# Reordering one first-transform piece and adding 14 idle products at the seam of a spectral filter and its hash-routed experts

## The chip, the cores and the metric

One core of one Trainium2 chip runs the whole program in one launch. The metric is the device time of that core in microseconds (us), as the median of the runs. Its engines are named as in the profile: PE (matrix products, with PEld for the loading of weights), DVE, ACT and POOL (element-wise work), SP (issue of transfers); ACT and POOL issue transfers as well. All transfers share 16 DMA engines.

## The reference

Eight sequences of 2496 tokens with 256 channels are filtered in the frequency domain; then every token goes through one of eight experts, which its id chooses.

```python
X = np.fft.rfft(x, axis=1)
y = np.fft.irfft(X * (filt_r + 1j * filt_i)[None], n=x.shape[1], axis=1)
x = y.reshape(B * S, D)                       # 19968 tokens, D = 256
expert_idx = token_ids * np.int64(2654435761) % np.int64(E)     # E = 8
for e in range(E):
    xe = x[expert_idx == e]
    out[expert_idx == e] = np.maximum(xe @ w1[e], 0.0) @ w2[e]  # F = 1024
```

All of it is in float32.

## The kernel before

**The filter.** A sequence ("batch", class `Batch`, L219) is transformed by two small discrete transforms, 2496 = 39 x 64. Stage 1 (`stage1`, L280) multiplies pieces of the input by a table `wf_t`; there are six pieces (u = 0 to 5) of four columns each, the last one shorter. A piece is four matrix products of 256 columns into two PSUM tiles "pa" (`products`, L253), each followed by an ACT copy to a slot of `mid` (L269). Only the second piece of a pair (u = 1, 3) writes its pair to DRAM (`d`, L297), and for the third and fourth batch that write can be put off (list `put_off`, L293). Stage 2 loads `d` again (`load2`, L299), multiplies by a second table ("pb", L312), by the filter on DVE (L318 to L323) and by the way back ("pc", L335). Stage 3 (`stage3`, L417) makes the last products "pd" (L261, L267), which ACT copies to a tile `o`, and POOL then scatters the rows of `o` to their expert's place in the DRAM array `xs` by indirect DMA (`scatter`, L432). The first two batches turn their data on PE instead of going through DRAM (`turn4`, L382, "pu" and the DVE copies "t", L398 and L401).

**The experts.** The rows of `xs` are worked off in blocks of 256 tokens. `load` (L835) gathers a block by four transfers `xg` and one transfer `no` of the row numbers; for block 0 SP issues three of them and ACT two, for block 1 SP issues all, later blocks are ACT's. DVE transposes the block (`token_parts`, L852, "xt") and makes sums ("st", L868). `up` (L880) has 28 products of 128 columns into the banks a, b, c with DVE sums and ACT activations ("ht", L891) between them; `down` (L917) has 16 products of 256 columns ("dps", L922). `up` asks for the block after the next one right after its first ACT copy (L899, `ask`): the five transfers of that block stand in ACT's queue ahead of the four activations. The first block may start when all rows of the first two batches lie in `xs`.

**What sets the order.** The order is written out by hand: every piece of work has a due time in a list, the list is sorted (L819), and the pieces with a negative time, here `head` less 200 (L797), run ahead of the experts. Each engine then runs its own instructions strictly in that order, with waits on semaphores where one engine needs another. Around the change the list is: third batch's stage 1 with its last pieces at 119 and 121 (L789), second batch's last piece of stage 3 (u = 5) at 123 (L788), fourth batch's first four pieces of stage 1 at 123 to 123.3 (L796), `begin` at 123.5 and the loads of blocks 0 and 1 at 123.6 (L790), the put-off writes of the third batch at 124 (L791), its `load2` at 125 (L792), the put-off writes of the fourth batch at 126 (L794). A transfer counts on one of eight semaphores ("lanes") of its kind, in the order of the list as built, and an issue that takes a lane waits until the transfer that had the lane before has landed.

`warm` (L757) exists before as well: it is called once at the program's very start and multiplies the identity by itself into bank a.

```python
def warm(n):
    ps = banks["a"].tile([P, 4, P], F32, name="warm", tag="a")
    for k in range(n):
        nc.tensor.matmul(out=ps[:, k % 4, :], lhsT=ident[:], rhs=ident[:], start=True, stop=True)
```

Of the kernel before, what the change touches and what calls it, by code (L numbers as in the profile page):

```python
# [125 lines left out]
def kernel(  # L126
# [630 lines left out]
# [6 lines that stand above are left out]
    third = batches[2]  # L763
    head = [(0, lambda: warm(14))]
# [28 lines left out]
    fourth = batches[3]  # L793
    head += [(126, lambda: [nc.sync.dma_start(out=dram, in_=chip) for dram, chip in put_off[3]])]  # L794
    head += [(t, lambda v=v: fourth.load1(v)) for v, t in enumerate((113, 113.1))]
    head += [(123 + .1 * u, lambda u=u: fourth.stage1(u)) for u in range(4)]  # L796
    todo = [(t - 200, piece) for t, piece in head]  # L797
    todo += [(t, lambda k=k: pads(k)) for k, t in enumerate((10.9, 11.6, 11.9, 16.9, 17.6, 17.95, 22.9))]

# [16 lines left out]
    for e in range(E):  # L816
        t = 34.3 + 1.5 * e
# [313 lines left out]
```

## Time and profile before

| what | value |
|---|---|
| three runs | 1421.33, 1423.53, 1431.88 us; median 1423.53 us |
| the profiled execution | 1424.24 us, its span 1422.5 us |
| PE busy | 1373.4 us (97% of the span) |
| PEld busy | 1273.3 us (90%) |
| DVE, POOL, ACT busy | 890.2, 830.3, 416.6 us |
| mean granted clock of PE | 0.99 |
| chain that ended last | 86% PE, 8% DMA, 3% DVE |
| PE busy from 100 to 150 us | 42.55 of 50 us, granted clock 0.93 |
| PE busy from 150 to 175 us | 21.91 of 25 us, granted clock 0.86 |
| PE busy from 250 to 325 us | 75 of 75 us, granted clock 1.00 |

How to read it: times in the views are us from the start of the span. A timeline line gives start, duration, engine, line, operation, "output<-input" and, in brackets, how long the engine was idle before it and what ended that. An fp32 product shows as two records, so "x8" is four products. "PEclk" and the clock column are the share of its full speed that PE was granted: 1.00 or 0.50, or a mean over a slice with both.

### The profile page before, as it was taken

How to read it: one execution, taken by the hardware profiler on the slowest of the kernel's cores; microseconds unless marked ns; L12 is line 12 of the kernel's file. 1: busy time of each engine (PE TensorE's matmuls, PEld its weight loads, DVE VectorE, ACT ScalarE, POOL GpSimd, SP SyncE). 2: the span in 40 equal slices, each digit the busy share in tenths (PEclk: the TensorE clock that was granted, in tenths of full speed). 3: DMA queues.
4: the chain of work that ended last, by engine and by line, in shares of the span. 5: the costliest groups of instructions: out<-in, count | busy, mean ns of one | idle time of the engine just before them, and what ended most of it. 6: DMA issues, size and time to landing. Idle time of an engine off the chain costs nothing.

```text
span 1422.5 us, 26307 instructions
## 1 busy us (share of the span) xinstructions
PE 1373.4 (97%) x9398; PEld 1273.3 (90%) x9398; DVE 890.2 (63%) x1636; ACT 416.6 (29%) x760; POOL 830.3 (58%) x736
## 2 busy tenths in 40 slices
PE   7898999999999999999999999999999999999997
PEld 7776888989888988889999899999999999999997
DVE  7773575575556566445665477657766776676775
ACT  4554122223232223232222222222222222222222
POOL 6167243844665565578533587788855566555563
PEclk9999899999999999999999999999999999999999
DMA  8677765757987698888755785887742526261611
GB/s 222 206 235 216 212 218 121 260 192 245 269 270 224 183 284 264 261 262 273 241 167 131 219 258 170 235 242 235 254 138 68 190 62 199 46 218 42 215 46 35
DMA packets 244505, 278.33 MB, mean 196 GB/s; under 512 B 125171, under 2 KB 213670, under 8 KB 234948
## 3 DMA queue, kind: packets, MB, share of 16 engines
q1 hardware_dynamic: 95149, 179.33, 40.2%
q10 hardware_dynamic: 129303, 52.69, 15.4%
q0 software_dynamic: 19920, 44.59, 8.9%
q8 instruction: 77, 1.26, 0.4%
q14 instruction: 56, 0.46, 0.1%
HBM read 293.65 MB, written 86.15 MB: 267 GB/s over the span
## 4 chain that ended last, share of the span: by engine, by line
PE 86%; DMA 8%; DVE 3%; issue 1%; ACT 1%; ACTq 0%; SPq 0%; POOLq 0%; POOL 0%; DVEq 0%
PE dps L922 22%; PE up_b L887 9%; PE up_a L887 6%; PE up_c L887 6%; PE pd L267 5%; PE pb L312 4%; PE dnc L949 4%; PE dnb L949 4%; PE dna L949 4%; PE upc L944 4%; PE upa L944 4%; PE pc L335 3%; PE pa L267 3%; DMA t<-d 2%; PE upe L944 2%; PE upb L944 2%
## 5 line engine op out<-in xcount | busy, mean ns | idle before, releaser
L922 PE MATMUL dps<-wts,ht 128*128 128x256 f32 x1600 | 370.9, 382 | 6.1 <-ACT ht L891 6.1
L922 PEld LDWEIGHTS dps<-wts,ht 128*128 128x128 f32 x1600 | 304.7, 192 | 50.6 <-ACT ht L891 7.3
L1014 POOL DMA_INDIRECT out_dram<-osb,no x158 | 165.2, 1046 | 219.2 <-DVE osb L956 137.8
L433 POOL DMA_INDIRECT xs<-o,sidx x176 | 177.0, 1006 | 168.7 <-ACT o L269 73.3
L877 POOL TENSOR_TENSOR tw<-wts 128x512 f32<-128x512 f32 x158 | 205.1, 1298 | 116.0 <-DMA wts<-in_moe_w_dram 92.4
L877 POOL TENSOR_TENSOR tw<-wts,tw 128x512 f32<-128x512 f32 x158 | 206.1, 1305 | 6.2
L894 DVE TENSOR_TENSOR ht<-up_b,ht 128x512 f32<-128x512 f32 x150 | 103.7, 691 | 114.6 <-PE up_b L887 91.2
L891 ACT ACTIVATE ht<-ht 128x512 f32<-128x512 f32 x150 | 94.3, 630 | 188.8 <-DVE ht L894 164.9
L322 DVE TENSOR_TENSOR z<-pb,filt 64x512 f32<-64x512 f32 x160 | 110.2, 689 | 30.9 <-PE pc L335 28.9
L927 DVE COPY osb<-dps 128x512 f32<-128x512 f32 x50 | 34.6, 691 | 150.2 <-PE dps L922 149.7
L887 PE MATMUL up_a<-xt,wts 128*128 128x128 f32 x800 | 115.3, 277 | 9.1 <-DVE xt L855 4.9
L887 PEld LDWEIGHTS up_a<-xt,wts 128*128 128x128 f32 x800 | 105.9, 193 | 12.7 <-DVE xt L855 5.3
L887 PE MATMUL up_b<-st,tw 128*128 128x128 f32 x800 | 107.4, 278 | 2.7 <-DVE ht L894 1.8
L887 PEld LDWEIGHTS up_b<-st,tw 128*128 128x128 f32 x800 | 98.1, 193 | 4.9 <-issue 3.7
L953 ACT ACTIVATE ht<-ht 128x512 f32<-128x512 f32 x90 | 56.6, 630 | 122.1 <-DVE ht L956 75.8
L894 DVE TENSOR_TENSOR ht<-up_c,ht 128x512 f32<-128x512 f32 x100 | 69.0, 690 | 37.2 <-PE up_c L887 32.4
L338 ACT COPY mid<-pc 128x512 f32<-128x512 f32 x60 | 35.0, 584 | 154.8 <-PE pc L335 91.5
L267 PE MATMUL pd<-t,wi_t 120*117 120x256 f32 x320 | 77.5, 385 | 2.6 <-DMA t<-d 2.6
L318 DVE TENSOR_TENSOR y<-pb,filt 128x512 f32<-128x512 f32 x80 | 55.1, 689 | 37.8 <-PE pb L312 35.6
L269 ACT COPY o<-pd 117x512 f32<-117x512 f32 x80 | 45.0, 585 | 104.4 <-DMA xg<-xs 45.4
L312 PE MATMUL pb<-mid,d_t 128*128 128x256 f32 x280 | 74.1, 388 | 1.1 <-DVE z L322 1.1
L898 ACT COPY ht<-up_a 128x512 f32<-128x512 f32 x50 | 29.3, 587 | 150.6 <-PE up_a L887 120.7
(210 smaller groups left out, 2466.1 us busy)
## 6 DMA issues: line engine op xcount, KB each, us to landing
wts<-in_moe_w_dram SPq DMA_DIRECT2D x162, 1024.0 KB
xg<-xs ACTq DMA_DIRECT2D x321, 64.0 KB
mid<-d SPq DMA_DIRECT2D x70, 256.0 KB
d<-mid ACTq DMA_DIRECT2D x60, 256.0 KB
d_t<-t2s SPq DMA_DIRECT2D x15, 1024.0 KB
e_t<-t2s SPq DMA_DIRECT2D x15, 1024.0 KB
x<-in_x_dram SPq DMA_DIRECT2D x39, 312.0 KB
t<-d SPq DMA_DIRECT2D x12, 960.0 KB
```

The costliest lines, as they stand in the source:

```text
L267: nc.tensor.matmul(out=ps[0:cols * H, k, :], lhsT=w[:], rhs=src[:, 2 * i + k, :], start=True, stop=True)
L312: nc.tensor.matmul(out=ps[:, i, :], lhsT=d_t[:, s, :], rhs=rhs, start=True, stop=True)
L322: nc.vector.tensor_tensor(out=z[b], in0=ps[a], in1=f_t[1][64 * hi:64 * hi + 64, s1:s1 + 2, :], op=OP.mult)
L433: st = nc.gpsimd.indirect_dma_start(out=xs[:], out_offset=bass.IndirectOffsetOnAxis(ap=index, axis=0), in_=rows, in_offset=None, bounds_ch ...
L877: eng.tensor_tensor(t[k][:], p, q, op=OP.subtract)
L887: nc.tensor.matmul(out=ps[bank][:, f, :], lhsT=w[:, f * P:(f + 1) * P], rhs=xx, start=first and f == 0, stop=True, skip_group_check=True)
L891: nc.scalar.activation(out=out, in_=in_, func=AF.Relu)
L894: nc.vector.tensor_tensor(out, ps[bank][:], other, op=OP.add)
L922: nc.tensor.matmul(out=ps[:, h, :], lhsT=ht[:, h, fp, :], rhs=w2[:, fp, :], start=(fp == 0), stop=(fp == FP - 1))
L944: nc.tensor.matmul(out=ps[:, f, :], lhsT=w[:, f * P:(f + 1) * P], rhs=xx, start=first and f == 0, stop=True, skip_group_check=True)
L949: nc.tensor.matmul(out=ps[:, 0, :], lhsT=a[:, f, :], rhs=b[:, f, :], start=first and f == 0, stop=True, skip_group_check=True)
L1014: st = nc.gpsimd.indirect_dma_start(out=out[:], out_offset=bass.IndirectOffsetOnAxis(ap=to_rows[i][:, h:h + 1], axis=0), in_=o[:, h, :], i ...
```

## The change

The first piece of the fourth batch's stage 1 gets the due time 121.5, ahead of the second batch's last piece of stage 3 at 123; the other three keep their order at 123.1 to 123.3. After them, still ahead of `begin`, stand 14 products of `warm`.

```diff
     head += [(t, lambda v=v: fourth.load1(v)) for v, t in enumerate((113, 113.1))]
-    head += [(123 + .1 * u, lambda u=u: fourth.stage1(u)) for u in range(4)]
+    head += [(t, lambda u=u: fourth.stage1(u)) for u, t in enumerate((121.5, 123.1, 123.2, 123.3))]
+    head += [(123.4, lambda: warm(14))]
     todo = [(t - 200, piece) for t, piece in head]
```

As built, PE has the four products of the piece ahead of the two of "pd" and 14 more ahead of the first "up_a"; ACT has the piece's two copies ahead of the two copies of `o`; DVE, POOL and SP have the same instructions in the same order. Ten of the 1286 transfers stand in the list, or count on a lane, otherwise than before: four in which two scatters of POOL and two input loads of SP change places in the list without a change of lane, and six around the gather of block 2. There the third and fourth transfer `xg` of block 2 and its `no` have other lanes: `no` counts on the lane of the first put-off write of the third batch (L791), where before it counted on that of block 2's own first `xg`.

## Prediction

> **What bounds the kernel now.** I read the page's busy shares and slices first:
>
> ```profile
> PE 1373.4 (97%) x9398; PEld 1273.3 (90%) x9398; DVE 890.2 (63%) x1636; ACT 416.6 (29%) x760; POOL 830.3 (58%) x736
> PEclk9999899999999999999999999999999999999999
> ```
>
> PE is the bound almost everywhere, so only idle or half-clocked PE time can be won, and only near the seam from 100 to 180 us, where a slice shows 8. There, second, the timeline of PE:
>
> ```profile
> 126.99 1.21 PE L261 MATMUL pd<-t,wi_t 120*117 120x256 f32 x4 [1.77 <-DVE t L401]
> 128.13 8.85 PE L267 MATMUL pa<-x,wf_t 117*120 117x256 f32 x32
> 141.85 2.08 PE L887 MATMUL up_a<-xt,wts 128*128 128x128 f32 x8 [4.87 <-DVE xt L855]
> ...
> 153.09 10.02 PE L922 MATMUL dps<-wts,ht 128*128 128x256 f32 x32 [3.12 <-ACT ht L891]
> ```
>
> Three gaps: 1.77, 4.87 and 3.12 us. Each is followed by slow products: "dps" took 10.02 us for 32 records, where full speed is 16 records in 3.45 us (chain, at 201.84), so 6.9. Third, one-microsecond windows (columns: stretch; PE, PEld, DVE, ACT, POOL busy; granted clock; DMA share; GB/s):
>
> ```profile
> 128.00:129.00 1.00, 1.00 (x3) 0.77 (x3) 0.87 (x4) 0.63 (x2) 0.69 (x2) 0.58 0.56 204
> 131.00:132.00 1.00, 1.00 (x5) 0.81 (x4) 1.00 (x2) 0.16 (x1) 0.70 (x2) 0.71 0.35 99
> ...
> 141.00:142.00 1.00, 0.15 (x1) 0.15 (x1) 0.88 (x2) 0.00 (x0) 1.00 (x2) 0.91 0.78 137
> 145.00:146.00 1.00, 1.00 (x9) 1.00 (x9) 0.39 (x1) 0.00 (x0) 0.00 (x0) 0.88 1.00 292
> ...
> 152.00:153.00 1.00, 0.00 (x0) 0.00 (x0) 0.37 (x2) 1.00 (x3) 0.00 (x0) 0.53 0.46 42
> 158.00:159.00 1.00, 1.00 (x4) 0.82 (x3) 0.00 (x0) 0.00 (x0) 0.00 (x0) 0.55 1.10 308
> ```
>
> From the fractions the clock is half from 128.17 to 131.58, 141.82 to 145.24 and 152.06 to 158.89: one, one and two steps of 3.41 us on one fixed grid. Judged by grid steps: 124.75 to 128.17 was 48% busy and a drop followed; 134.99 to 138.41 was 59% busy (work until 137.0) and none followed; 148.65 to 152.06 was 39% busy, a drop. So a step that is about half idle drops the clock, and a full step of work at half clock restores it.
>
> Fourth, what releases the first block ("up_a" at 141.85)? POOL's timeline and SP's:
>
> ```profile
> 135.26 0.90 POOL L433 DMA_INDIRECT xs<-o,sidx  x1 [0.30 <-ACT mid L269]
> 137.55 3.32 SPq L844 DMA_DIRECT2D xg<-xs  x7
> ```
>
> POOL scatters back to back, every 1.30 us, until 136.2; the last lands at 137.4 by the trace's DMA updates, SP gathers block 0 from 137.55, DVE transposes at 141.08. PE has no part in it. Fifth, what releases "dps" at 153.09? ACT's timeline:
>
> ```profile
> 144.18 5.53 ACTq L844 DMA_DIRECT2D xg<-xs  x4
> 151.47 0.40 ACTq L844 DMA_DIRECT2D no<-xs  x1
> 151.92 0.63 ACT L891 ACTIVATE ht<-ht 128x512 f32<-128x512 f32 x1 [7.37 <-DMA xg<-xs]
> ```
>
> The four activations stand behind block 2's `no`, which is not issued until 151.47 although its predecessor's issue ended at 149.71: it waits for its lane, whose last transfer, block 2's first `xg`, landed at 151.45.
>
> [...]
>
> **The change, part by part.**
>
> *The moved piece:* four products (1.73 us at full clock, as at 122.34) and two ACT copies of 0.59; no DMA, as only odd pieces write. PE ends the third batch's stage 1 at 125.22. The piece's input, the fourth batch's first x load, landed only at 126.40 by the DMA updates, so it runs from about 126.45 to 128.2, not from 125.22. "pd" was ready at 126.99 and now starts at 128.2: 1.2 us late. Behind "pd" are ACT's two copies of `o`, before at 128.24, now about 129.5, and behind those POOL's last two scatters at 133.97 and 135.26. Slack 133.97 - 130.1 = 3.9 us, so this costs nothing; the cover is POOL's backlog of scatters, and without it the cost is the 1.2 us. ACT's copies of `o` also pass the piece's two copies, 1.2 us, inside that slack. No queue of SP, DVE or POOL is passed.
>
> *The clock there:* the step 124.75 to 128.17 becomes 0.47 + 1.72 = 2.19 busy, 64%: no drop, 1.7 us of PE saved. Three pieces remain: 129.2 + 3 x 1.73 = 134.4 (their input x, landed by about 130.4, is in time at 130.9). Before: 137.0.
>
> *The 14 products:* eight records of this shape take 0.89 us ("up_b", chain), so 28 take 3.12: 134.4 to 137.5. They wait for nothing; bank a was free since the copies at 117.8. They end where PE ended before (137.0), 4.3 us ahead of "up_a". Cost nothing: they lie in the wait for POOL. Without that cover, 3.1.
>
> *The first block:* "up_a" still at 141.85. An idle stretch of 4.3 us leaves some grid step over half idle wherever the grid lies (at best 2.15 on each side, 63% of a step). So "up" is cold as before, end at 149.97. Gain to here: 0.
>
> *The lane:* as built, `no` of block 2 now waits for the first put-off write, which landed at 148.31, not for the `xg` landing at 151.45. Issue then at 149.75, after the fourth `xg`, 1.72 us sooner; activations at 150.2; "dps" at 151.37. The step 148.65 to 152.06 is then 1.32 + 0.69 busy, 59%: on the edge, as the step that did not drop. No drop makes "dps" 6.9 instead of 10.02, 3.1 more. PE stands 1.7 to 4.8 us ahead at the end of "dps".
>
> *What takes it back:* the fourth batch's fifth piece (L267, at 176.58) needs x loaded by SP:
>
> ```profile
> 176.58 1.96 PE L267 MATMUL pa<-x,wf_t 117*120 117x256 f32 x8 [0.31 <-issue]
> ```
>
> PE waited for x there already: the third x transfer landed at 176.38. It was issued at 173.15, when block 4's first `xg`, its lane's predecessor, had landed (173.13); the second at 170.36, when a put-off write of the fourth batch had landed (170.34), which PE doesn't move. With PE ahead that `xg` is issued up to 4.8 us earlier, so the third goes right behind the second, at 171.2, and with the same 3.2 us lands at 174.4: "pa" at 174.6, 2.0 us sooner. The rest of the lead becomes idle time: 176.27 - 4.8 = 171.5, so up to 3.1 us idle, over half of a step, and a new drop costs up to 3.41/2 = 1.7. Unknown bounds here: the third x may land at 174.4 (lead 2.0) or,[...] at 176.4 (lead 0). Later DVE stalls on the chain (0.85 at 187.79, 0.47 at 209.78) may shrink with a DVE that started earlier: 0 to 0.9 more. From 250 us on PE has no gap to hide in, so the lead at 240 reaches the end.
>
> Sum: lead 2.0, less half of the possible 1.7 for the drop (I can't tell from the edge case which), rounded with the DVE relief left out: 1.2 us. 1422.5 - 1.2 = 1421.3 of span; with 1.74 around it (1424.24 - 1422.5) 1423.0 for that execution. It stands 0.71 above the median 1423.53, so **1422.3** as a median.
>
> **Rivals.**
> *A. The products keep the clock up* through "up" and "dps": 1.7 + 3.4 less at the first block, and x in time too. For it: the drops at 141.82 and 152.06 are real. Against: 4.3 us idle after them. If POOL's chain came in about 2.5 us sooner it would hold. Time 1423.5 - 5 = 1418.5.
> *B. Slower: the lead turns into a cold stretch.* Place: the wait for the fifth piece's x. PE comes at 171.5, x stays at 176.4, the step 172.54 to 175.96 is empty, the clock drops. Price 1.7 us with nothing won: 1425.2. It decides once the wait exceeds half a step, 1.7 us, while x lands after 176. For it: x landing is paced by writes of the fourth batch, not by PE. Against: its third part has a lane that PE's lead frees.
> *C. Late "pd" holds the scatters.* It decides if x lands after 126.4 + 3.9 = 130.3; each us beyond is one us more, 1425 at 132. Against: 3.9 us of slack.
> *D. Nothing reaches the end*: the built order does move the piece, but all of it lies in waits, and the lane's 1.7 us goes into the wait for x: 1423.5.
>
> **How the numbers follow.** Forecast 0.45, A 0.12, B 0.2, C 0.05, D 0.18. About 1%, 14 us, is what a measurement of this kernel can tell from no change; all cases lie within 5 us. [...]each drop is 1.7 us, and the three runs shown spread from 1421.33 to 1431.88. The forecast's own range is 1420 to 1425; with A, B and that spread 1417.5 to 1427.5. Faster by over 1%: 0.01; within: 0.97; slower: 0.02.
>
> **What would show it.** In the profile after: no idle over 1.3 us at 125, "pd" about 1.2 us later, no half clock at 128 (grid permitting); the idle products ending near 137.5; "up_a" with 4 to 5 us idle before it, then half clock; POOL's last scatter at 135; `no` of block 2 issued right after its fourth `xg`; "dps" at about 151.4; a longer wait ahead of the fifth "pa". I am wrong if "up" runs at full clock from its start, if SP's gather of block 0 moves by over 1 us, or if PE's lead at 240 us exceeds 3 us.

## The result and the profile after

In its first measurement the changed kernel took 1418.74 us (median of 20 runs, 1412.59 to 1425.83) beside 1425.16 for the kernel before (20 runs): ratio 0.995, interval [0.9929, 0.9971]. A second measurement, on another occasion, gave 0.9974 [0.9956, 0.9992]. So it is 0.26 to 0.5% faster, some 4 to 7 us. (The ratios in this document, with their 95% intervals, are not the quotients of the medians beside them.) The forecast was 1.2 us. The gain is real, and most of it is not where the forecast looked.

The page of the profile after has PE's busy time 4.1 us lower, although 28 matmul and 28 weight-load records more are in it:

```profile
PE 1369.3 (97%) x9426; PEld 1271.4 (90%) x9426; DVE 891.9 (63%) x1636; ACT 416.0 (29%) x760; POOL 828.0 (59%) x736
PEclk9999999999999999999999999999999999999999
```

**At the seam** nearly every step went as written. PE's timeline after, from the moved piece on:

```profile
124.00 1.99 PE L267 MATMUL pa<-x,wf_t 117*120 117x256 f32 x8
125.82 1.15 PE L261 MATMUL pd<-t,wi_t 120*117 120x256 f32 x4
126.90 5.44 PE L267 MATMUL pa<-x,wf_t 117*120 117x256 f32 x24
132.18 3.29 PE L761 MATMUL warm<-ident 128*128 128x128 f32 x28
138.78 1.40 PE L888 MATMUL up_a<-xt,wts 128*128 128x128 f32 x8 [3.31 <-DVE xt L856]
...
148.09 7.17 PE L923 MATMUL dps<-wts,ht 128*128 128x256 f32 x32 [0.91 <-ACT ht L892]
```

The 1.77 us gap is gone, the idle products end 3.3 us ahead of "up_a", and "dps" waits 0.91 us instead of 3.12 and takes 7.17 us instead of 10.02. The reason for the shorter wait is in ACT's timeline: block 2's `no` follows right behind its fourth `xg`.

```profile
140.43 5.75 ACTq L845 DMA_DIRECT2D xg<-xs  x4
146.22 0.65 ACTq L845 DMA_DIRECT2D no<-xs  x1
146.92 0.63 ACT L892 ACTIVATE ht<-ht 128x512 f32<-128x512 f32 x1 [6.12 <-DMA xg<-xs]
```

And most of it is taken back at the fifth piece of the fourth batch's stage 1, as forecast:

```profile
171.46 1.96 PE L267 MATMUL pa<-x,wf_t 117*120 117x256 f32 x8 [3.03 <-issue]
```

To compare profiles whose starts differ by some us (SP's gather of block 0 began at 137.55 before and 134.40 after; unchanged kernels run again had 136.58 and 137.40, so that difference is not the change's), I count from that gather. To the start of block 5's "dps" (253.47 before) it is 115.9 and, in a second profile, 113.6 before, 113.4 and 114.3 after. Means 114.8 and 113.9: 0.9 us, within what two executions of one kernel differ by. And that 0.9 is not the seam's: up to the "pd" that starts at 240.26 before, the means are 102.4 and 102.3, and the first profile before has a half-clock step right behind it, at 240.8, which the other three don't have.

**Around 500 us** the two kernels differ by more, in code that the change doesn't touch. Before, from PE's timeline, then ACT's, then SP's:

```profile
502.35 2.56 PE L922 MATMUL dps<-wts,ht 128*128 128x256 f32 x8 [3.00 <-ACT ht L891]
```
```profile
499.45 0.31 ACTq L844 DMA_DIRECT2D xg<-xs  x1
500.75 0.38 ACTq L844 DMA_DIRECT2D no<-xs  x1
```
```profile
485.95 1.55 SPq L406 DMA_DIRECT2D t<-d  x1
487.62 0.47 SPq L303 DMA_DIRECT2D mid<-d  x1
```

After, the same three views:

```profile
497.05 1.99 PE L923 MATMUL dps<-wts,ht 128*128 128x256 f32 x8 [0.55 <-ACT ht L892]
```
```profile
494.26 0.31 ACTq L845 DMA_DIRECT2D xg<-xs  x1
```
```profile
483.10 0.39 SPq L406 DMA_DIRECT2D t<-d  x1
483.61 2.47 SPq L303 DMA_DIRECT2D mid<-d  x4
```

Read from the bottom up. SP's issue of the t transfer (load4 of batch 4) took 1.55 us before and 0.39 after. Behind it on SP stand four `mid` transfers (load2). The first of them landed at 499.43 before and 494.24 after, by the trace's semaphore updates: 14.0 and 11.7 us after SP's issue of the weights just ahead. ACT's fourth `xg` gather uses that transfer's semaphore again, and started 0.02 us after each landing (499.45, 494.26), although its third had been issued at 495.54 and 492.70. `no` followed the second `mid` in the same way (500.73, 500.75). The activations stand behind them on ACT, and PE behind those: 3.00 us idle. Then the clock halves, as one-microsecond windows show (granted clock is the third number from the end), before and after:

```profile
504.00:505.00 1.00, 1.00 (x4) 0.82 (x3) 0.00 (x0) 0.00 (x0) 0.17 (x1) 0.50 1.09 206
506.00:507.00 1.00, 1.00 (x4) 0.78 (x3) 0.35 (x1) 0.00 (x0) 0.00 (x0) 0.50 1.07 356
```
```profile
499.00:500.00 1.00, 1.00 (x7) 0.85 (x6) 0.80 (x5) 0.00 (x0) 0.94 (x1) 1.00 1.09 225
```

Price, estimated from these lines: 3.00 - 0.55 us of waiting and half of one 3.41 us step, 1.7 us: 4.2 us. Not all of the later landing is the issue: of the 2.3 us (14.0 less 11.7) about half is the longer issue; the other half lies in the first `mid` transfer itself, which took 11.8 us from issue to landing before and 10.6 after. These runs don't show why.

What slows the issue? The share of each DMA queue in a window from 485.5 to 487.5 of the kernel before, and from 482.5 to 485 of the changed one (queue: packets, MB, share):

```profile
q1 hardware_dynamic: 21, 0.17, 48.4%
q8 instruction: 1, 0.02, 3.6%
```
```profile
q1 hardware_dynamic: 38, 0.31, 51.8%
q0 software_dynamic: 2, 0.00, 0.5%
```

One packet of 16,384 B on q8, a queue whose kind the page gives as "instruction", began at 485.94, 0.01 us before SP's issue; I take such a packet for an instruction fetch. In the changed kernel it began at 480.80, 2.3 us ahead of the issue. The page counts such packets:

```profile
q8 instruction: 77, 1.26, 0.4%
```

TensorE's records number 19,290 (19,346 after), 251 per packet, and no other engine has a quarter of that, so I take q8 for TensorE's fetches; this is an estimate from the counts. In the changed kernel 28 more records of matmul and 28 of weight load stand in that stream, ahead of everything behind the seam. PE itself hardly shows the fetches: in the profile before, it was busy for over 90% of the packet's time in 76 of the 77. SP's issues do: over all fourteen profiles of this study, 336 issues of t transfers at L406, 37 began between 0.2 us ahead of and 0.4 us behind the start of a q8 packet (bounds set with the traces at hand). Their median was 1.46 us, and 26 took over 1 us; of the other 299 the median was 0.39, and 6 took over 1 us. The 37 are not independent: most stand at three places of the program, at about 230, 485 and 775 us.

The same traces tell more than a coincidence. All 26 long issues end 0.43 to 0.57 us after the end of the fetch's packet, 25 of them 0.43 to 0.46, although the packets took from 0.92 to 1.44 us; at 485 us, in the seven profiles with the collision, it is 0.43 each time. The fetches there are no longer for it: 1.00 to 1.44 us in these seven, 0.96 to 1.49 in the five unswapped profiles without. So it is the issue that is drawn out until the fetch has ended, and not the other way round. Other issues show the same: of ACT's `no` 25 of 31 within those bounds took over 1 us (3% of the others), all of them ending 0.35 to 0.60 us after the packet; of SP's `mid` 30 of 37 (7% of the others); of SP's loads of weights none of 44.

### The profile page after: what moved, and what is told of

It is laid out like the page before. It is cut to its first block, busy times and chain, and to the rows that moved or that the text cites. A ratio compares the mean times of both kernels' runs of the same rounds, so it can differ in the third digit from the quotient of the medians.

```text
span 1413.3 us, 26363 instructions
## 1 busy us (share of the span) xinstructions
PE 1369.3 (97%) x9426; PEld 1271.4 (90%) x9426; DVE 891.9 (63%) x1636; ACT 416.0 (29%) x760; POOL 828.0 (59%) x736
## 4 chain that ended last, share of the span: by engine, by line
PE 82%; DMA 8%; DVE 4%; issue 2%; ACT 1%; POOL 1%; ACTq 1%; SPq 0%; POOLq 0%; DVEq 0%
PE dps L923 20%; PE up_b L888 8%; PE up_a L888 5%; PE up_c L888 5%; PE pd L267 4%; PE dnc L950 4%; PE dnb L950 4%; PE dna L950 4%; PE upc L945 4%; PE upa L945 4%; PE pb L312 4%; PE pa L267 3%; PE pc L335 3%; PE upe L945 2%; PE upb L945 2%
## 5 line engine op out<-in xcount | busy, mean ns | idle before, releaser
L923 PE MATMUL dps<-wts,ht 128*128 128x256 f32 x1600 | 367.0, 380 | 1.5 <-ACT ht L892 1.5
L888 PE MATMUL up_a<-xt,wts 128*128 128x128 f32 x800 | 114.8, 276 | 7.3 <-ACT ht L899 4.0
L323 DVE TENSOR_TENSOR y<-y,z 128x512 f32<-128x512 f32 x80 | 73.6, 920 | 2.7
```

Of the source, the lines that this page charges most:

```text
L888: nc.tensor.matmul(out=ps[bank][:, f, :], lhsT=w[:, f * P:(f + 1) * P], rhs=xx, start=first and f == 0, stop=True, skip_group_check=True)
L923: nc.tensor.matmul(out=ps[:, h, :], lhsT=ht[:, h, fp, :], rhs=w2[:, fp, :], start=(fp == 0), stop=(fp == FP - 1))
```

## The experiments

The first four vary the two parts of the change and the number of products.

**e1, the moved piece alone.** The line with `warm(14)` at 123.4 is left out.

> The moved piece alone, no idle products; as built, the transfers of block 2 count on the lanes they had before, so its row-number transfer waits for its own first gather again. Lane theory: dps of block 0 starts about 3 us after the end of up, as before (3.12 us idle), and the median stays within 2 us of before. Clock theory: the half-clock stretch at 128 us is gone and PE is done 3 to 4 us sooner than before ahead of the first up_a, but idle longer there; a gain of 1 to 2 us if the drop at 128 mattered at all. Theory that POOL's scatter chain came in sooner because of the move: SP's gather of block 0 starts 2 us or more sooner than before relative to POOL's first scatters, gain 3 us or more.

Measured: 1420.89 us beside 1423.17, ratio 0.9995 [0.9976, 1.0013]. No gain.

**e2, the products alone.**

```diff
-    head += [(t, lambda u=u: fourth.stage1(u)) for u, t in enumerate((121.5, 123.1, 123.2, 123.3))]
+    head += [(123 + .1 * u, lambda u=u: fourth.stage1(u)) for u in range(4)]
```

> The 14 idle products alone, no moved piece; as built, the lanes are those of the changed kernel. Lane theory: block 2's row-number transfer is issued right behind its fourth gather, dps of block 0 starts under 1.5 us after up, 3 to 5 us gained up to there, and the median is 3 to 6 us under before although nothing was moved. Clock theory: the products end close to the first up_a (about 140 us), so up runs mostly at full clock and gains 1.7 us in addition. Move theory: no gain, within 2 us of before.

Measured: 1419.72, ratio 0.996 [0.9942, 0.9978]. Nearly the whole gain without the move.

**e3 and e4, the move with 8 and with 24 products** (`warm(8)`, `warm(24)`).

> The change with 8 idle products in place of 14; as built the lanes are those of the changed kernel. Lane theory: the same gain as the change, 5 to 7 us. Clock theory: 1.3 us fewer of idle products leave a longer gap ahead of up_a, a gain smaller by 1 to 2 us.

Measured: 1424.34, ratio 1.0007 [0.9985, 1.0028].

> The change with 24 idle products in place of 14 (5.35 us of them); as built the lanes are those of before. Lane theory: most of the gain goes, dps of block 0 waits about 3 us for ACT again, the median within 2 us of before. Clock theory: the products end 1 to 2 us ahead of up_a, so up and the products behind it run at full clock: a gain of 6 us or more, larger than the change's.

Measured: 1419.1, ratio 0.9966 [0.995, 0.9981].

As built, block 2's `no` has its new predecessor in e2 and e3, its old one in e1 and e4. e3 has the new one and gains nothing, e4 the old one and gains: my lane step is not where the gain comes from, although e2 came out as the lane theory said. The clock theory fails too: in e4 it had its way, with no half-clock step from 115 to 190 us, and the gain is no larger than the change's. What goes with the gain is the number of instructions added to TensorE's stream (0 and 32 without gain, 56 and 97 with), and in the profiles the slow issue, the wait and the half-clock stretch at 500 us: all three in e1 and e3, none in e2 and e4. From this came the theory FETCH, with its rival SEAM (the products gain by clock and buffers where they stand). The next four separate count from place. As built, every DMA has the semaphore that it has in the kernel before (g1, g4) or in the changed one (g2, g3).

**g1, 56 instructions more at the very start, seam untouched.**

```diff
-    head = [(0, lambda: warm(14))]
+    head = [(0, lambda: warm(28, 64))]
```

with `warm(n, m)` using `ident[:, :m]` on both sides. The 56 matmul records took 5.31 us where 28 took 5.22.

> The kernel before, nothing changed at the seam; its 14 idle products at the very start (64 instructions' worth in TensorE's stream stay in place after them) are cut into 28 of 64 columns, so that TensorE's stream is 56 instructions longer from there on, as it is in the changed kernel after the seam. Theory FETCH (TensorE's 16 KB instruction fetches fall at other places, and the one at about 485 us no longer meets SP's issue of the t transfer): that issue takes 0.4 us instead of 1.5, the multiplication at about 502 waits under 1 us for its activation, no half-clock stretch at 503 to 507, median 3 to 5 us under the kernel before (ratio 0.9965 to 0.998). Theory SEAM (the gain is made by the products at the seam, by clock and buffers there): as the kernel before, ratio 0.999 to 1.001, with the wait and the half-clock stretch at 500 to 507.

Measured: 1416.01 beside 1422.71, ratio 0.9961 [0.9944, 0.9978]. As FETCH said; SEAM's 0.999 to 1.001 lies outside the interval. From SP's timeline and PE's:

```profile
483.94 0.39 SPq L406 DMA_DIRECT2D t<-d  x1
```
```profile
497.73 1.99 PE L922 MATMUL dps<-wts,ht 128*128 128x256 f32 x8 [0.40 <-ACT ht L891]
```

At the seam g1 looks like the kernel before: "up_a" at 141.98, "dps" at 153.12 after a wait of 2.99, half clock from 152.3 to 159.1. All that the change does there is missing, and the time is won.

**g2, the changed kernel with the same PE time in half the instructions**: 7 products of 256 columns (`rhs=e_t[:, 0:2, :]`), 3.19 us.

> The changed kernel with its 14 idle products at the seam as 7 products of 256 columns: about the same 3.1 us of TensorE at the same place, but 28 instructions in its stream instead of 56. Theory FETCH: the shift of 28 is under the 32 with which the collision at about 485 us was still there, so SP's issue of the t transfer takes 1.5 us or more again, the multiplication at about 500 waits 2 to 3 us, the clock halves at 500 to 507, and most of the gain is gone: ratio 0.998 to 1.0005. Theory SEAM: as the changed kernel, ratio 0.994 to 0.997.

Measured: 1420.96, ratio 0.998 [0.9958, 1.0003], at the lower end of what FETCH gave and above SEAM's, though the interval reaches into both. The trace has the late issue and the wait again, but no half-clock stretch behind it:

```profile
480.43 1.41 SPq L406 DMA_DIRECT2D t<-d  x1
```
```profile
497.11 1.99 PE L930 MATMUL dps<-wts,ht 128*128 128x256 f32 x8 [3.29 <-ACT ht L899]
```

**g3, 8 products' work as 16 of 64 columns** (`warm(16, 64)`, 2.08 us).

> The changed kernel with the work of 8 idle products at the seam (which gave nothing in e3), as 16 products of 64 columns: 64 instructions instead of 32, in about the same 1.8 us of TensorE. Theory FETCH: shift 64, past the collision (it was gone at 56 and 96): issue 0.4 us, no wait of over 1 us and no half-clock stretch at 500 to 507, ratio 0.994 to 0.9975. Theory SEAM: as e3, ratio 0.999 to 1.002.

Measured: 1418.65, ratio 0.9972 [0.995, 0.9994]. The time lies inside FETCH's range, but not for FETCH's reason: the trace shows the collision, which I had expected to be gone at 64. The fetch at 481.69 met the issue at 481.70, which took 1.67 us, and "dps" waited 3.57 us, with the half clock after it. So "over 32" is no rule: 0, 28, 32 and 64 more collide, 56 and 97 don't.

**g4, the control for g1: 32 instructions more at the start** (`warm(22, 96)`).

> The kernel before with its 14 idle products at the very start cut into 22 of 96 columns: 32 instructions more, as in e3, nothing changed at the seam. A control for g1. Theory FETCH: with a shift of 32 the collision at about 485 us is still there (issue 1.5 us or more, wait and half-clock stretch at 500 to 507), ratio 0.998 to 1.002. Theory SEAM: ratio 0.999 to 1.001 too. If it gains as g1 is to gain, recutting the products at the start is itself the cause, and neither theory holds.

Measured: 1420.91, ratio 0.998 [0.9961, 0.9999]. Collision (1.95 us), wait (2.18) and half clock are there, and half of g1's gain. So by the ratios alone, recutting the products at the start is not excluded as a part of the cause. The table below helps: both kernels recut them, and where the wait at 500 us stands g4 takes 17.1 us and g1 13.6.

The last four take the collision away without touching TensorE's stream, and repeat the two kernels.

**h1 and h2, one pair on SP's queue swapped**, in the kernel before and in the changed one:

```diff
-        out += part3(b, a3, [max(e0, a3[2 * v] - 2.2) for v in range(NV)])
+        out += part3(b, a3, [max(e0, a3[2 * v] - 2.2) - .3 * (b == 4 and v == 0) for v in range(NV)])
```

> The kernel before with one pair swapped on SP's queue at about 485 us: the t transfer (load4 of batch 4, piece 0) is issued ahead of the weights' load that it stood behind, so it starts 2 to 3 us earlier and can no longer be issued in the moment of TensorE's instruction fetch. TensorE's stream and the seam are as before. Theory FETCH with its chain (fetch slows the t issue, the four mid transfers behind it are issued and land late, the fourth xg gather and the no gather of the block wait for them on the same DMA semaphore, the activation is late, TensorE waits and its clock halves): the fourth gather starts within 1.5 us of the third instead of 3.4 later, TensorE's wait at about 502 is under 1 us, no half-clock stretch there, ratio 0.9955 to 0.998. Rival (the late t issue is a mark of such executions, and the time is lost or won elsewhere): wait gone or not, ratio 0.999 to 1.001.

Measured: 1419.65 beside 1421.67, ratio 0.9992 [0.9966, 1.0017] (14 runs). In the trace the chain came apart as FETCH said: the t issue took 0.39 us, the fourth gather followed 0.49 us after the third, "dps" waited less than 0.15 us, no half clock. The time did not follow: a miss for FETCH as I put it, inside the rival's range.

> The changed kernel with the same swap. Theory FETCH: in the changed kernel the collision is already gone, so the swap adds little: ratio 0.993 to 0.997, as the changed kernel's 0.995 within 0.2%. Rival (seam and swap are worth something each by themselves): 0.990 to 0.993.

Measured: 1421.0, ratio 0.999 [0.9972, 1.0007], above the changed kernel's 0.9974 in the same comparison (h4), and outside both expectations. The swap moves some twenty later transfers of SP and ACT to other semaphores (by the semaphores in the traces), and a wait for DVE stands in both swapped profiles some 50 us later, at the same "pb" product. In h1 and h2, from PE's timeline:

```profile
553.74 1.10 PE L312 MATMUL pb<-mid,d_t 128*128 128x256 f32 x4 [1.91 <-DVE z L322]
```
```profile
543.98 1.63 PE L312 MATMUL pb<-mid,d_t 128*128 128x256 f32 x4 [1.90 <-DVE z L322]
```

In the four profiles of the two unswapped kernels it is at most 0.43 us. In h2 the clock halves there too (544.4 to 547.8). So the gain is given back at the next wait; the table below shows how much of it.

**h3 and h4, the two kernels once more.**

> The kernel before once more, unchanged, for a second profile and as a test of the measurement. Theory FETCH: SP's t issue at about 485 us takes 1.5 us or more again, the wait and the half-clock stretch at 500 to 507 are there again. If the collision is a matter of chance from execution to execution, it may be absent. Ratio 0.9985 to 1.0015 in either case.

Measured: 1423.45, ratio 1.0005 [0.9983, 1.0027]; issue 1.73 us, wait 2.38, half clock from 500.7 to 504.1.

> The changed kernel once more, unchanged, for a second profile and a second ratio. Theory FETCH: t issue 0.4 us, no wait of over 1 us and no half-clock stretch at 500 to 507; ratio 0.994 to 0.997. Rival (chance in that one profile): the collision is there with unchanged ratio.

Measured: 1418.54, ratio 0.9974 [0.9956, 0.9992]; issue 0.39 us, wait 0.24, no half clock; the ratio is just above the expected range. The pattern belongs to the program, not to the execution.

All kernels together. PE runs the same products in the same order in all fourteen profiles, but for the idle ones and the moved piece, so the traces can be laid beside each other product by product. "Distance" is SP's t issue less the start of the nearest fetch. "Stretch" runs from the last "up_b" ahead of that "dps" (498.29 before) to the next "up_a" (516.23), "next" from there to the "up_a" at 563.81.

| kernel | instructions added | distance, us | t issue, us | wait of "dps", us | stretch, us | next, us | ratio |
|---|---|---|---|---|---|---|---|
| before, h3 | 0 | 0.01, 0.06 | 1.55, 1.73 | 3.00, 2.38 | 17.9, 17.3 | 47.6, 48.1 | 1, 1.0005 |
| e1 | 0 | 0.01 | 1.74 | 2.14 | 17.1 | 47.6 | 0.9995 |
| e3 | 32 | -0.09 | 1.74 | 2.44 | 17.4 | 48.1 | 1.0007 |
| g4 | 32 (start) | -0.08 | 1.95 | 2.18 | 17.1 | 47.6 | 0.998 |
| g2 | 28 | 0.01 | 1.41 | 3.29 | 16.5 | 47.8 | 0.998 |
| g3 | 64 | 0.02 | 1.67 | 3.57 | 18.5 | 48.8 | 0.9972 |
| after, h4 | 56 | 2.31, 2.32 | 0.39, 0.39 | 0.55, 0.24 | 13.8, 13.5 | 48.2, 47.6 | 0.995, 0.9974 |
| e2 | 56 | 2.33 | 0.39 | under 0.15 | 13.4 | 47.6 | 0.996 |
| g1 | 56 (start) | 2.30 | 0.39 | 0.40 | 13.6 | 47.7 | 0.9961 |
| e4 | 97 | 6.51 | 0.39 | 0.52 | 13.8 | 48.9 | 0.9966 |
| h1 | 0, swapped | over 7 | 0.39 | under 0.15 | 13.0 | 51.2 | 0.9992 |
| h2 | 56, swapped | over 7 | 0.39 | under 0.15 | 13.0 | 51.6 | 0.999 |

Over the twelve unswapped profiles the stretch takes 17.4 us in the mean with the collision and 13.6 without: 3.8 us, and the two groups don't overlap, whatever was done at the seam. Outside of it they hardly differ: 360.0 and 359.6 us from the gather of block 0 to the stretch, 48.0 and 48.0 next, 857.7 and 857.0 from there to the end. The swap saves as much in the stretch, and 3.2 to 3.6 us of it are gone in the next 50 us; so the ratios near 1 of h1 and h2 are no evidence against the chain, but they show that a wait removed there need not reach the end.

With collision the seven ratios have the mean 0.9991, without it the five unswapped ones have 0.9962: 0.29%, 4.1 us. (With h1 and h2 the free ones have 0.9970.) Within the colliding rows the untouched seams (before, h3, g4) have the mean 0.9995, the others 0.9989; within the free rows g1, with an untouched seam, has 0.9961, the others 0.9963. Each ratio is known to about 0.2%, 3 us, so these means alone don't measure the seam; the traces do better. From the gather of block 0 to the "pd" at 240.26, the six unswapped profiles with the old lane take 102.4 us in the mean, the six with the new one 102.5: by 240 us nothing is left of the lane's gain.

## Why the prediction was right and where it was not

The direction, the bound of 1% and the mechanism at the seam held; the size did not: 1.2 us were forecast, some 4 to 7 measured. The median of 1418.74 lies below the 1420 to 1425 given for the forecast itself, inside the wider range that the rivals and the spread opened. That the direction came out right is luck for the most part: the forecast gain at the seam is not there by 240 us, and what gained was not in the forecast.

- *The moved piece*: held. It ran without a gap, earlier than forecast (its x was there by 124.00 in that execution), "pd" lost nothing and no drop followed at 128. But none of the other five profiles with the piece in its old place (h3, e2, g1, g4, h1) has a drop there either, so the one that the piece was to prevent belonged to one execution. Alone it gains nothing (e1).
- *The 14 products*: held as to their own time: 3.29 us by their row, all inside the wait for POOL. What their instructions did further on is the subject of the failed step, below.
- *The first block*: held. "up" began cold in both profiles after, half clock from 139.5 and from 141.2. The sign "wrong if SP's gather of block 0 moves by over 1 us" was badly chosen: it moved by 3.15 us in one profile after and by 0.15 in the other, since executions differ by that much.
- *The lane*: held. From "up_a" to "dps" it took 11.24 and 11.17 us before, 9.31 and 9.40 after: 1.8 us, where 1.72 was forecast. To the product behind that "dps", 21.10 and 19.87 became 16.32 and 16.42: a lead of 3.5 to 4.8, inside the 1.7 to 4.8.
- *What takes it back*: held. PE waited 3.03 us at the fifth piece and 2.44 in h4, there with a half-clock step after it (175.4 to 178.8). It took back all of the lead, not most of it: nothing is left at 240 us, where 1.2 was forecast; these runs can't tell the two apart.
- *Rivals*: A did not come about, since "up" stayed cold; in e4 it did, and gained no more than the change. B and C did not come about, and D describes the seam about as well as the forecast does.

The failed step is the last sentence of the working, "from 250 us on PE has no gap to hide in, so the lead at 240 reaches the end". It takes the rest of the program as fixed but for a shift. It was not, and the figure behind it, PE busy in 75 of 75 us, ends at 325 us: there was a 3 us wait at 502, and the change removed it. The sum lacks a term of about -4 us, which comes not from the time of the 14 products but from their instructions. Nothing in the diff points at 500 us, but the trace before shows the place: the longest wait of PE between 250 and 1400 us, with a half-clock step behind it and an issue of 1.55 us at its root where the median of that line is 0.39.

What is shown: the gain lies in one stretch of 18 us, where the profiles with and without the collision fall into two groups (16.5 to 18.5 us and 13.0 to 13.8). It comes with 56 more instructions at the start as it does with 56 at the seam (g1). In all seven collisions at 485 us the slow issue ends 0.43 us after the fetch. Behind it, the late landing of the `mid` transfers holds ACT's gathers and so PE (in the kernel before the first landed at 499.43, the fourth gather was issued at 499.45, and PE was idle for 3.00 us until 502.35). Not shown by an experiment: that a fetch placed at will slows an issue; no run did that, and making the fetch start later without changing the stream was not tried. Open: why 64 instructions collide and 56 don't, why the `mid` transfer took longer, and why g2, g3 and g4 took 0.2 to 0.3% less time with the collision present (the intervals of g2 and g4 reach to 1 or nearly). The number of instructions is no simple rule either: at about 775 us the fetch begins within 0.2 us of a t issue in twelve of the fourteen profiles, with 0, 28, 32, 56 and 64 instructions more.

## What to carry to other kernels

What instructions added to an engine's long stream cost or gain need not be their own time. Here, with 56 more in TensorE's, at the seam or at the program's start, the fetch near 485 us began 2.3 us ahead of SP's t issue instead of within 0.1 us of it, the issue took 0.39 us instead of 1.41 to 1.95, and a stretch of 17.4 us in the mean took 13.4 to 13.8; with 64 more, in g3, it did not come about. So a gain or loss under half a per cent is to be tested with a control that has the same number of instructions elsewhere, before it is credited to the place where they stand. When a change moves the time by more than its own stage can give, lay the two traces beside each other product by product and look for the first stretch that differs, however far away.

## What the runs showed of the hardware

- SP's issue of a t transfer (40 to 960 KB) took 1.46 us (median of 37) where it began between 0.2 us ahead of and 0.4 us behind the start of a 16 KB instruction fetch, and 0.39 us elsewhere (median of 299). All 26 long ones ended 0.43 to 0.57 us after the fetch. Of ACT's `no` issues 25 of 31 were over 1 us there, of SP's loads of weights none of 44.
- At about 500 us ACT's fourth gather, whose semaphore an earlier `mid` transfer still had, was issued 0.02 us after that transfer's last landing in both kernels: 3.4 us of idle queue between the third gather's issue and the fourth's in the kernel before, 0.8 in the changed one.
- Waits of 2.1 to 3.6 us ahead of "dps" were followed by a 3.41 us half-clock step in six of seven profiles; one of 3.29 us (g2) was not, nor the 3.03 us at the fifth piece in the changed kernel.
- Matmul records of 64 columns took 65 ns each in g3 (2.08 us for 32), those of 128 columns 117 ns (3.29 for 28), those of 256 columns 228 ns (3.19 for 14).
